# Attention and mixture of experts on one core: the sums of weights behind the centroids' products, and what follows one turn later

## The chip, the cores and the metric

The kernel runs on one core of one Trainium2 chip. The metric is the device time of one execution in microseconds (us); the median of ten executions is 711.23 us. A core has five engines that run their own instruction queues and wait for each other through semaphores: PE (TensorE, matmuls into PSUM), DVE (VectorE), ACT (ScalarE), POOL (GpSimd) and SP (SyncE, which here only issues DMAs). Each engine works through its own queue strictly in order. An instruction that waits therefore holds up everything behind it on its engine.

## The reference

Attention first, over 4 batches, 8 heads, 768 positions and a head size of 64. Queries and keys are assigned to one of 16 centroids of their head, and a query sees only keys of its own centroid:

```python
q_assign = np.argmax(np.einsum('bhsd,hcd->bhsc', q_n, c_n), axis=-1)
k_assign = np.argmax(np.einsum('bhsd,hcd->bhsc', k_n, c_n), axis=-1)
mask = q_assign[:, :, :, None] == k_assign[:, :, None, :]
scores = np.where(mask, scale * np.matmul(q, k.transpose(0, 1, 3, 2)), -1000000000.0)
attn = np.exp(scores - np.max(scores, axis=-1, keepdims=True))
attn = attn / (np.sum(attn, axis=-1, keepdims=True) + 1e-09)
x = np.matmul(attn, v)
```

The result, as 3072 rows of 512, goes to a mixture of 8 experts: a cosine router picks one expert for each row, and the row becomes `gate * (relu(x @ w1[e]) @ w2[e])`. The change touches only the attention part.

## The kernel before, in words

**Pairs, turns, units.** The attention part runs over 16 pairs n = 0 to 15: a batch and two heads. A pair has two groups (the two halves of the queries), and a group has six units (six blocks of 128 keys). The main loop takes two units a turn, so a pair has six turns, `it` = 0 to 5: the first group ends in turn 2, the second in turn 5. The names in the profile are those of the code; L numbers are lines of the kernel before.

**One turn.** Each engine's order is written out by hand: it is the order in which the loop emits instructions (`manual_schedule` over all five). A turn emits, in this order: some loads on SP; `scores` and `expo` of the next turn's two units; `between(n, it)`, which holds everything that isn't plain attention; the routing of early rows in some turns of batches 2 and 3 (`early`); and `attend` for this turn's two units.

- `scores` (L484) makes a unit's scores on PE: four bf16 matmuls that add the mask out of the tile H ("hot" in the profile), then f32 matmuls with qT and kT. The array works as four tiles of 64*64. The result goes to one of two PSUM tiles s_ps.
- `expo` (L495) is the exponential on ACT, out of s_ps into one of five buffers `prob`. A buffer is free when the unit five before has been attended and added up.
- `attend` (L506) multiplies prob with v on PE, in 64*64 tiles, into o_ps. There is one o_ps tile, so it is used by one group after the other. On DVE the same function adds prob into acc (L515 for a group's first two units, L525 after that). When a group ends, ACT copies o_ps to o_sb (L530).
- `unite` (L539) adds the halves of o_sb into o_sum on POOL, in turns 2 and 5.

**What prepares a pair** (`prep_pieces`). "turn0" and "turn1" turn q and k into qT and kT by 32x32 blocks on DVE (L386). "products" multiplies qT and kT with the centroids on PE, in tiles of 128*32 (L396), and turns the result on DVE into asn (L405). "choose" finds the nearest centroid with four DVE instructions (L414 to L417, amax, sel, sel, pm), writes three small copies into cd on ACT (L419, L422), and lets SP issue a transposing DMA from cd into H (L427). H, qT and kT have two buffers each. H of pair n + 1 is first needed in turn 5 of pair n.

**What ends a pair.** `total` sums acc over its partitions on PE, for both groups of the pair before, with matmuls against ones in tiles of 128*32 (L553); DVE turns the sums (L570) and takes the reciprocal (L571), and POOL spreads it with eight small copies to inv2 (L574). `divide` turns inv2 into den (L585) and multiplies o_sum with it into xT (L589) on DVE. `rows` turns xT into xb (L606) and issues four stores on SP into x_rows (L613). The last group's sums are taken alone, with a reciprocal of 384 columns (L562).

**Shared PSUM.** products, total and the router's matmuls share two PSUM banks ("misc"), used alternately. `route_pieces` belongs to the router of a finished batch: its products (L628, copied by ACT at L636) and logits (L641, reduced by DVE at L644) come in the first two pairs of the next batch.

**Order before.** For pairs n > 0: turn 0 has products for n + 1, then the attend, then total of n - 1; turn 1 has choose for n + 1; turn 2 ends with divide of n - 1 and unite; turn 3 has rows of n - 1; turn 4 has turn0 for n + 2, and turn 5 turn1. Pair 0 differs: turns 0 to 2 hold the turns, the products and choose of pair 1.

**Loads.** SP issues the loads of v for n + 1 in turn 2 (eight DMAs), of q for n + 3 in turn 4 and of k in turn 5 (four each), all at the head of their turn. In pairs 11 to 15 it also issues the first experts' weights.

Of the kernel before, what the change touches and what calls it, by code (L numbers as in the profile page):

```python
# [34 lines left out]
def bc(ap, shape, axis):  # L35
    return ap.unsqueeze(axis).to_broadcast(shape)
# [3 lines left out]
def kernel(  # L40
# [136 lines left out]
    def misc():  # L177
        return bank("misc", psM)

    pairs = [(b, hp) for b in range(B) for hp in range(NHP)]  # L180
    NP = len(pairs)
# [131 lines left out]
    def turned_experts():  # L313
        bk = misc()
        for c in range(KD):
            nc.tensor.transpose(
                bk[:, E * c : E * c + E], emb[:, P * c : P * c + P], ident[0:E, 0:E]
            )
        nc.vector.tensor_copy(
            embT[:, :, 0:E], bk[:, 0 : KD * E].rearrange("p (c e) -> p c e", e=E)  # L320
        )
# [210 lines left out]
    def unite(g):  # L532

        n, hq, _ = units[GU * g]
        t = ld[n]
        if hq == 0:
            t["o_sum"] = xp.tile([P, 2, HE], F32, tag="o_sum", name="o_sum", bufs=2)
        add = (nc.gpsimd if n + 1 < NP else nc.vector).tensor_tensor
        add(t["o_sum"][:, hq], t["o_sb"][:, 0], t["o_sb"][:, 1], ALU.add)  # L539

    def total(*gs):

        g = gs[0]
        d = gr[g]
        n = units[GU * g][0]
        G = len(gs)
        bk = misc()

        M, W = (D, HS) if G == 1 else (D // 2, HS // 2)
        for i in range(P // M):  # L550
            for k, g in enumerate(gs):
                c = i * W % HS
                nc.tensor.matmul(  # L553
                    bk[M * i : M * i + M, W * k : W * k + W],
                    lhsT=ones[:, 0:M],
                    rhs=gr[g]["acc"][:, i * W // HS, c : c + W],
                    start=True,
                    stop=True,
                )
        den = d["den"] = smp.tile([P, G, HS], F32, tag="den", name="den", bufs=1)  # L560
        if G == 1:
            nc.vector.reciprocal(den[:, 0], bk[:, 0:W])  # L562
            return


        U = W // SQ
        sums = smp.tile([P, G * U, SQ], F32, tag="sums", name="sums", bufs=1)
        inv = smp.tile([P, G, U], F32, tag="inv", name="inv", bufs=1)
        inv2 = d["inv2"] = smp.tile([P, G, 2, U], F32, tag="inv2", name="inv2", bufs=1)
        nc.vector.transpose(sums.rearrange("p g i -> p (g i)"), bk[:, 0 : G * W])  # L570
        nc.vector.reciprocal(inv.rearrange("p k u -> p (k u)"), sums[:, :, 0])  # L571
        for i in range(4):
            for to in (i, i ^ 1):
                nc.gpsimd.tensor_copy(  # L574
                    inv2[M * to : M * to + M, :, i % 2], inv[M * i : M * i + M]
                )

    def divide(*gs):
        n, hq, _ = units[GU * gs[0]]
        d = gr[gs[0]]  # L580
        G = len(gs)
        if hq == 0:
            xT[pairs[n]] = xp.tile([P, 2, HS], F32, tag="xT", name="xT", bufs=4)
        if G == 2:
            nc.vector.transpose(  # L585
                d["den"].rearrange("p k (u t) -> p (k u) t", t=SQ),
                bc(d["inv2"].rearrange("p k h u -> p (k h u)"), [P, G * HS // SQ, SQ], 2),
            )
        nc.vector.scalar_tensor_tensor(  # L589
            out=xT[pairs[n]][:, hq : hq + G],  # L590
            in0=ld[n]["o_sum"][:, hq : hq + G, 0:HS],
            scalar=ld[n]["o_sum"][:, hq, HS:HE],
            in1=d["den"],
            op0=ALU.add,
            op1=ALU.mult,
        )
        for g in gs:
            gr[g].clear()
# [473 lines left out]
    def expert_of(it):  # L1072
        table = {"early": e_early, "sized": e_sized, "block": e_block, "whole": e_block}[it.kind]
        return nc.values_load(
            table[0:1, it.j : it.j + 1], engines=(EngineType.SP,), min_val=0, max_val=E - 1
        )
# [247 lines left out]
    def piece(n, name, *args):  # L1324
        if n < NP:
            if n not in prepare:
                prepare[n] = prep_pieces(n)
            prepare[n][name](*args)

    def between(n, it):  # L1330
        b, nb = divmod(n, NHP)
        if n == 0:

            if it == 0:
                piece(1, "turn0")
                piece(1, "turn1")
            elif it == 1:
                piece(1, "products")
            elif it == 2:
                piece(1, "choose")  # L1340
                turned_experts()
            elif it == 3:
                later_constants()
        elif it == 0:
            piece(n + 1, "products")
        elif it == 1:
            piece(n + 1, "choose")
        elif it == 3:
            rows(2 * n - 2, 2 * n - 1)
        if it == 4:  # L1350
            piece(n + 2, "turn0")
        elif it == 5:
            piece(n + 2, "turn1")
        if b > 0:
            if nb == 0 and it == 3:
                route[b - 1] = route_pieces(b - 1)
            products, logits, read, norms, choose = route.get(b - 1, (None,) * 5)


            m = NJ * nb + it  # L1360
            if m in (8, 11, 14):
                read((m - 8) // 3 * 2, (m - 8) // 3 * 2 + 2)
            if m in (15, 16, 18, 19, 21, 22):
                norms((15, 16, 18, 19, 21, 22).index(m))
            if (nb, it) == (0, 4):
                products(0)
            elif (nb, it) == (0, 5):
                products(1)
            elif (nb, it) == (1, 2):
                logits(0)  # L1370
            elif (nb, it) == (1, 3):
                logits(1)
            elif (nb, it) == (1, 4):
                choose()
        if n == NP - 1 and it == 4:
            route[b] = route_pieces(b)
            route[b][2](0, NJ, 0, P - SQ)
        first = {
            (11, 3): (w1s, 0, 0),
            (12, 3): (w1s, 0, 1),  # L1380
            (13, 3): (w2s, 0, 0),
            (14, 3): (w2s, 0, 1),
            (14, 4): (w1s, 1, 0),
            (15, 0): (w1s, 1, 1),
            (15, 1): (w2s, 1, 0),
            (15, 2): (w2s, 1, 1),
        }
        if (n, it) in first:
            w, j, i = first[n, it]
            own = E0[j]  # L1390
            if own.e is None:
                own.e = expert_of(own)
            x, chunks = (moe_w1, KD) if w is w1s else (moe_w2, KF)
            load_part(w[own.slot], x, own.e, chunks, i, 2)
# [9 lines left out]
    with tc.manual_schedule(engines=by_hand):  # L1404
        begin()
        for i in range(0, len(units), 2):
            n, it = divmod(i // 2, NJ)

            if n == it == 0:
                load(2, "qk")  # L1410
            if it == 2 and n + 1 < NP:
                load(n + 1, "v")
            if it >= 4 and n + 3 < NP:
                load(n + 3, "qk"[it - 4])
            for m in range(i + 2, min(i + 4, len(units))):
                scores(m)
                expo(m)
            between(n, it)
            if it == 4 and n == NP - 1:
                divide(2 * n)  # L1420
            b, nb = divmod(n, NHP)
            if (b, nb, it) in early:
                early[b, nb, it]()
            if i + 2 == len(units):
                ats.close()
                tile_waits = {"side": "right", "reuse_waits": "tile"}
                psX = ctx.enter_context(tc.tile_pool(name="psX", bufs=1, space=PSUM, **tile_waits))
                turn_x(E0[0], nc.scalar.copy, xp.tile([P, DM], F32, tag="acc", name="xTm", bufs=3))
            for m in range(i, i + 2):
                attend(m)  # L1430
            if it == 2:
                if n > 0:
                    divide(2 * n - 2, 2 * n - 1)
                unite(2 * n)
            elif it == 5:
                unite(2 * n + 1)
            if i + 2 == len(units):
                rows(ngroups - 2)
                route[b][0](0)
            if it == 0 and n > 0:  # L1440
                total(2 * n - 2, 2 * n - 1)
            elif it == 3 and n == NP - 1:
                total(2 * n)
        at.close()
        mop = ctx.enter_context(tc.tile_pool(name="mop", bufs=2, **tile_waits))
# [193 lines left out]
```

## Time and profile before

| what | value |
|---|---|
| median of 10 runs | 711.23 us (711.06 to 712.62) |
| the profiled execution | 711.25 us, its span 709.4 us |
| granted TensorE clock, mean | 0.997 |
| PE busy | 694.8 us (98% of the span) |
| DVE, ACT, POOL busy | 381.2, 268.3, 264.8 us |
| scores L484 (f32 part), 1536 matmuls | 156.1 us |
| attend L506, 1536 matmuls | 142.6 us |
| acc L525 on DVE, 128 instructions | 125.1 us |
| reciprocal spread L574 on POOL, 120 copies | 42.9 us |

The span begins with the first instruction and ends with the last; the time has a little around it. In a timeline a line gives the start in us, the duration, engine, line, operation, what is written and read, and how many instructions were merged; the brackets give the idle time of the engine ahead of it and what ended it. Matmuls of different array tiles run side by side, so durations in a merged line overlap; the distance between starts is the better measure.

### The profile page before, as it was taken

The numbers are of one execution on the slowest core, as the hardware profiler recorded it, in microseconds if no ns is written. First come the engines' busy times: TensorE is split into PE (matmuls) and PEld (weight loads), VectorE is DVE, ScalarE is ACT, GpSimd is POOL, SyncE is SP. The second block draws the span as 40 slices with busy tenths as digits, with TensorE's granted clock in tenths as the row PEclk, the third lists the DMA queues.
The fourth block names the chain that finished last, engine by engine and source line by source line (L and its number), as shares of the span: only waits on it lengthen the run. The fifth ranks groups of instructions, "written<-read, shape, count | busy, mean of one in ns | idle before, by whom it ended". The sixth has DMA issues, their size and how long they took to land.

```text
span 709.4 us, 16021 instructions
## 1 busy us (share of the span) xinstructions
PE 694.8 (98%) x6462; PEld 454.6 (64%) x6462; DVE 381.2 (54%) x665; ACT 268.3 (38%) x454; POOL 264.8 (37%) x402
## 2 busy tenths in 40 slices
PE   6999999999999999999999999999999999999995
PEld 3444444444444444444876668897979797979793
DVE  4788887998979998998684111340120303031210
ACT  4566665577556656666415110101011111111110
POOL 2122222222224221354043546736264454545412
PEclk9999999999999999999999999999999999999998
DMA  9636665866548687769698987268768686869450
GB/s 147 93 63 107 105 104 86 152 146 116 99 75 160 123 158 154 125 190 356 124 340 313 347 322 265 70 247 287 260 211 298 210 301 234 313 243 330 142 197 29
DMA packets 244123, 135.53 MB, mean 191 GB/s; under 512 B 207808, under 2 KB 207810, under 8 KB 244044
## 3 DMA queue, kind: packets, MB, share of 16 engines
q1 hardware_dynamic: 237852, 121.28, 63.9%
q0 software_dynamic: 6016, 13.12, 5.3%
q8 instruction: 53, 0.87, 0.5%
q14 instruction: 26, 0.21, 0.1%
q10 hardware_dynamic: 176, 0.05, 0.0%
HBM read 115.92 MB, written 13.12 MB: 182 GB/s over the span
## 4 chain that ended last, share of the span: by engine, by line
PE 83%; DVE 5%; issue 5%; DMA 4%; POOL 1%; ACT 0%; POOLq 0%; SPq 0%; DVEq 0%; ACTq 0%
PE s_ps L484 19%; PE o_ps L506 16%; PE h_ps L1259 10%; PE y_ps L1275 10%; PE h_ps L1174 9%; PE y_ps L1209 5%; PE misc L1209 5%; PE x_ps L1174 3%; DMA out_dram<-ys,spidx 3%; DVE acc L525 2%; PE misc L553 2%; PE misc L396 2%; PE misc L628 1%; DMA k<-in_k_dram 1%; POOL out_dram L1050 1%
## 5 line engine op out<-in xcount | busy, mean ns | idle before, releaser
L495 ACT ACTIVATE prob<-s_ps 128x768 f32<-128x768 f32 x192 | 153.5, 811 | 93.5 <-PE s_ps L484 72.8
L484 PE MATMUL s_ps<-qT,kT 64*64 64x384 f32 x1536 | 156.1, 482 | 0.0
L506 PE MATMUL o_ps<-prob,v 64*64 64x385 f32 x1536 | 142.6, 487 | 0.0
L525 DVE TENSOR_TENSOR acc<-acc,prob 128x768 f32<-128x768 f32 x128 | 125.1, 977 | 8.5 <-DVE acc L525 0.5
L506 PEld LDWEIGHTS o_ps<-prob,v 64*64 64x64 f32 x1536 | 54.2, 133 | 70.6 <-issue 59.2
L1218 DVE STREAM_TRANSPOSE ys<-y_ps 128x256 f32<-128x256 f32 (+4 forms) x16 | 6.7, 416 | 153.3 <-PE y_ps L1209 153.3
L1259 PEld LDWEIGHTS h_ps<-xTm,w1s 128*128 128x128 f32 x768 | 87.4, 192 | 2.3 <-issue 1.6
L1259 PE MATMUL h_ps<-xTm,w1s 128*128 128x128 f32 x768 | 88.3, 275 | 0.0
L539 POOL TENSOR_TENSOR o_sum<-o_sb 128x385 f32<-128x385 f32 x30 | 32.1, 1071 | 149.5 <-ACT o_sb L530 149.5
L1050 POOL DMA_INDIRECT out_dram<-ys,spidx x56 | 57.0, 1018 | 74.5 <-DVE ys L1234 59.6
L1275 PE MATMUL y_ps<-w2s,hT 128*128 128x512 f32 x192 | 84.5, 593 | 0.0
L484 PEld LDWEIGHTS s_ps<-qT,kT 64*64 64x64 f32 x1536 | 56.4, 133 | 37.6 <-issue 34.6
L1174 PE MATMUL h_ps<-xTs,w1s 128*128 128x272 f32 (+7 forms) x384 | 72.9, 346 | 0.8 <-ACTq L1539 0.8
L1174 PEld LDWEIGHTS h_ps<-xTs,w1s 128*128 128x128 f32 x384 | 66.6, 190 | 8.1 <-issue 2.9
L1266 ACT ACTIVATE hT<-h_ps 128x512 f32<-128x512 f32 x24 | 14.3, 596 | 143.7 <-PE h_ps L1259 143.7
L484 PE MATMUL s_ps<-hot 64*64 64x384 bf16 x768 | 64.9, 325 | 2.3 <-ACT prob L495 1.3
L1039 POOL DMA_INDIRECT xs<-x_rows,gpidx x56 | 57.2, 1021 | 17.1 <-issue 16.8
L574 POOL COPY inv<-inv 32x12 f32<-32x12 f32 x120 | 42.9, 358 | 55.0 <-DVE inv L571 50.6
L1275 PEld LDWEIGHTS y_ps<-w2s,hT 128*128 128x128 f32 x192 | 35.6, 190 | 40.2 <-issue 40.2
L484 PEld LDWEIGHTS <-hot 64*64 64x64 bf16 x768 | 23.8, 107 | 39.7 <-issue 38.4
L1209 PE MATMUL y_ps<-hTs,w2o 128*128 128x272 f32 (+7 forms) x256 | 48.0, 346 | 0.0
L1209 PE MATMUL misc<-hTs,w2o 128*128 128x272 f32 (+7 forms) x256 | 48.0, 346 | 0.0
(264 smaller groups left out, 687.4 us busy)
## 6 DMA issues: line engine op xcount, KB each, us to landing
w1s<-in_moe_w_dram SPq DMA_DIRECT2D x18, 2048.0 KB, 10.6
w2s<-in_moe_w_dram SPq DMA_DIRECT2D x18, 2048.0 KB, 14.5
v<-in_v_dram SPq DMA_DIRECT2D x128, 48.0 KB, 2.1
q<-in_q_dram SPq DMA_DIRECT2D x60, 96.0 KB, 3.5
k<-in_k_dram SPq DMA_DIRECT2D x60, 96.0 KB, 3.5
x_rows<-xb SPq DMA_DIRECT2D x60, 96.0 KB, 2.9
xr<-x_rows SPq DMA_DIRECT2D x9, 512.0 KB, 4.0
w1s<-in_moe_w_dram SPq DMA_DIRECT2D x4, 1024.0 KB, 9.8
```

The lines of the kernel that those rows point to most:

```text
L484: nc.tensor.matmul(s_ps[D * half : D * half + D, h, 0:HS], lhsT=l[rows, half], rhs=r[rows], start=part == (1 if len(parts) < 2 else 0), st ...
L495: nc.scalar.activation(d["prob"][:, :, 0:HS], d["s_ps"][:, :, 0:HS], ACTF.Exp, scale=scale)
L506: nc.tensor.matmul(g["o_ps"][D * h : D * h + D, half, 0:HE], lhsT=ld[n]["v"][keys, j, h], rhs=d["prob"][keys, h, 0:HE], start=(j == 0), st ...
L525: nc.vector.tensor_tensor(g["acc"], g["acc"], d["prob"][:, :, 0:HS], ALU.add)
L539: add(t["o_sum"][:, hq], t["o_sb"][:, 0], t["o_sb"][:, 1], ALU.add)
L574: nc.gpsimd.tensor_copy(inv2[M * to : M * to + M, :, i % 2], inv[M * i : M * i + M])
L1039: nc.gpsimd.indirect_dma_start(out=to, out_offset=None, in_=of, in_offset=bass.IndirectOffsetOnAxis(ap=at, axis=0), bounds_check=n - 1, oo ...
L1050: inst = nc.gpsimd.indirect_dma_start(out=to, out_offset=bass.IndirectOffsetOnAxis(ap=at, axis=0), in_=of, in_offset=None, bounds_check=n - 1,
L1174: nc.tensor.matmul(bk, lhsT=w1s[it.slot][:, c, P * f : P * f + P], rhs=d["xT"][:, c, 0:C], start=(c == 0), stop=(c == KD - 1),)
L1209: nc.tensor.matmul(bks[g][:, 0:C], lhsT=d["w2"][:, f, P * g : P * g + P], rhs=d["hT"][:, f, 0:C], start=(f == 0), stop=(f == KF - 1),)
L1259: nc.tensor.matmul(bk[:, m : m + P], lhsT=w1s[it.slot][:, c, f0 + m : f0 + m + P], rhs=d["xT"][:, P * c : P * c + P], start=(c == 0), stop ...
L1275: nc.tensor.matmul(bk, lhsT=d["hT"][:, P * c : P * c + P], rhs=w2s[it.slot][:, c], start=(c == 0), stop=(c == KF - 1),)
```

## The change

Products for the next pair move from turn 0 to turn 1, and total of the pair before comes directly behind them, ahead of the attend of turn 1. Choose goes from turn 1 to 2, divide from the end of turn 2 to that of turn 3, rows from turn 3 to 4, the turn of q from 4 to 5, the turn of k from 5 to turn 0 of the next pair. The router's products go one turn later too. unite stays in turns 2 and 5.

```diff
         elif it == 0:
+            piece(n + 1, "turn1")
+        elif it == 1:
             piece(n + 1, "products")
-        elif it == 1:
+            total(2 * n - 2, 2 * n - 1)
+        elif it == 2:
             piece(n + 1, "choose")
-        elif it == 3:
+        elif it == 4:
             rows(2 * n - 2, 2 * n - 1)
-        if it == 4:
+        if it == 5:
             piece(n + 2, "turn0")
-        elif it == 5:
-            piece(n + 2, "turn1")
...
-            if (nb, it) == (0, 4):
+            if (nb, it) == (0, 5):
                 products(0)
-            elif (nb, it) == (0, 5):
+            elif (nb, it) == (1, 0):
                 products(1)
...
             if it == 2:
-                if n > 0:
-                    divide(2 * n - 2, 2 * n - 1)
                 unite(2 * n)
+            elif it == 3 and n > 0:
+                divide(2 * n - 2, 2 * n - 1)
             elif it == 5:
                 unite(2 * n + 1)
...
-            if it == 0 and n > 0:
-                total(2 * n - 2, 2 * n - 1)
-            elif it == 3 and n == NP - 1:
+            if it == 3 and n == NP - 1:
                 total(2 * n)
```

## The prediction

> **What bounds the kernel now.** I read the page first, for the engine that carries the time, and then the timeline of the attention part, since the change touches only that (it ends near 338 us).
>
> ```profile
> PE 694.8 (98%) x6462; PEld 454.6 (64%) x6462; DVE 381.2 (54%) x665; ACT 268.3 (38%) x454; POOL 264.8 (37%) x402
> PE 83%; DVE 5%; issue 5%; DMA 4%; POOL 1%; ACT 0%; POOLq 0%; SPq 0%; DVEq 0%; ACTq 0%
> ```
>
> PE sets the end. In the timeline of PE, a turn in which nothing else runs goes from one first matmul of the scores to the next in 2.91 us (182.38 to 185.29). The next view is the timeline of the pair that begins at 195.89: its turn 0, and the head of its turn 1.
>
> ```profile
> 195.89 0.34 PE L484 MATMUL s_ps<-hot 64*64 64x384 bf16 x4
> ...
> 197.62 0.52 PE L396 MATMUL misc<-qT,cnB 128*32 128x384 f32 x2
> ...
> 198.40 1.52 PE L506 MATMUL o_ps<-prob,v 64*64 64x385 f32 x16
> 198.61 0.58 DVE L405 STREAM_TRANSPOSE asn<-misc 128x384 f32<-128x384 f32 x1 [2.69 <-ACT prob L495]
> ...
> 199.85 0.88 PE L553 MATMUL misc<-acc,ones 128*32 128x192 f32 x16
> 200.66 0.36 PE L484 MATMUL s_ps<-hot 64*64 64x384 bf16 x4
> 200.90 0.58 DVE L570 STREAM_TRANSPOSE sums<-misc 128x384 f32<-128x384 f32 x1 [0.87 <-PE misc L553]
> 201.51 0.23 DVE L571 RECIPROCAL inv<-sums 128x12 f32<-128x12 f32 x1
> 201.66 0.50 DVE L414 TENSOR_REDUCE amax<-asn 128x24 f32<-128x384 f32 x1
> ...
> 203.76 0.40 ACT L419 ACTIVATE cd<-pm,wcd 128x24 bf16<-128x24 bf16 x1 [0.41 <-DVE pm L417]
> ```
>
> PE interrupts its 64*64 work twice in turn 0: for the centroids' products (L396) and, behind the attend, for the sums (L553). `choose` starts right behind the reciprocal, and its copies on ACT (L419, L422) come in turn 1, when ACT has nothing urgent behind them. DVE is nearly full here (50.82 us busy of 58.00 between 36 and 94 us); PE is not held up.
>
> The last view is that of the first pair, whose `choose` already stands in turn 2, where the change puts all of them.
>
> ```profile
> 22.66 1.52 PE L506 MATMUL o_ps<-prob,v 64*64 64x385 f32 x16
> ...
> 25.20 0.55 DVE L414 TENSOR_REDUCE amax<-asn 128x24 f32<-128x384 f32 x1
> ...
> 27.36 0.40 ACT L419 ACTIVATE cd<-pm,wcd 128x24 bf16<-128x24 bf16 x1 [0.68 <-DVE pm L417]
> ...
> 28.22 0.80 ACT L530 COPY o_sb<-o_ps 128x770 f32<-128x770 f32 x1
> ...
> 29.08 1.52 PE L506 MATMUL o_ps<-prob,v 64*64 64x385 f32 x16
> ```
>
> The copy of the finished group out of o_ps (L530) stands behind cd on ACT, and the next group's first attend (29.08), which writes the one o_ps tile, starts only when that copy is done.
>
> **The gain: PE enters another shape once instead of twice.** Turns 0 and 1 of a pair take 4.76 + 2.93 us, 1.88 over two plain ones. The matmuls are four passes of 192 columns and two of 384; a pass of 384 takes 0.32 (16 attend matmuls, four passes, in 1.29), so 1.30 is work and 0.58 is going in and out twice, 0.29 a visit. With the sums directly behind the products one visit's 0.29 goes. No row shows the step from products to sums; it costs between 0 and 0.29, and I take 0.02, as the step from bf16 to f32 inside the scores shows next to none: 0.27 saved. There are 14 pairs with both (n = 1 to 14; the last pair has no products): 14 x 0.27 = 3.8 us.
>
> **The loss: choose in turn 2 holds up the copy of o_ps.** Turn 2 is the one whose second unit ends the first group, so its attend is followed by the copy on ACT; `choose` stands before that attend in the program, so cd precedes the copy on ACT. cd waits for DVE, and DVE has in its order now: turn of the products (L405), turn of the sums, reciprocal, two acc of turn 1, and only then choose. Counted from N, the start of the attend in turn 1:
>
> - The chain: sums start at N + 0.17 (323.24 to 323.41 in the last pair), 0.61 to the reciprocal, 0.15 to acc, 2.05 for two acc, 2.10 from choose to cd (201.66 to 203.76), 0.86 to the copy (27.36 to 28.22), 0.80 for it, 0.06 to the matmul (29.02 to 29.08): N + 6.80.
> - PE without a wait: 1.35 to turn 2 (22.66 to 24.01), 2.91 to turn 3, 1.62 through its scores to the attend (182.38 to 184.00): N + 5.88.
>
> PE is held 0.92 us. A held attend also costs 0.05 more: in the first pair I work out a wait of 0.04 and the turn is 0.10 longer (3.01 against 2.91). So 0.97. The two acc are taken from the last pair, where they follow the reciprocal directly and the eight copies of inv run on POOL meanwhile, as they will everywhere:
>
> ```profile
> 324.02 0.23 DVE L571 RECIPROCAL inv<-sums 128x12 f32<-128x12 f32 x1
> 324.17 4.16 DVE L525 TENSOR_TENSOR acc<-acc,prob 128x768 f32<-128x768 f32 x4
> 324.31 4.30 POOL L574 COPY inv<-inv 32x12 f32<-32x12 f32 x8 [1.49 <-DVE inv L571]
> ```
>
> The lower bound is the first pair's own chain, without sums and without POOL: 29.08 - 22.66 = 6.42, so 0.54 + 0.05. This holds in full for n = 1 to 4, 6 to 8 and 10 to 12: 10 x 0.97 = 9.7. Pairs 5, 9 and 13 have logits (L641, 0.63 a turn) in turns 2 and 3 ahead of that attend; these 1.26 us of PE work cover the wait. Pair 14 has the early items' tokens (0.54) there: 0.4 is left. Together 10.1 us.
>
> Here a rule of the Trainium skill speaks against the change. On the page "SBUF — State Buffer", section "Who interferes with whom", a VectorE instruction with two SBUF inputs and a GpSimd instruction that reads SBUF exclude each other, and the one that comes second blocks fully. The rows above agree that they disturb each other, but here GpSimd is the one that loses: its eight copies take 4.30 instead of 3.07 us, an acc 1.04 instead of 0.97. Were each of the two acc held a whole copy of 0.38 us, the sum would be some 7 us higher.
>
> **What is given back.** Pairs 10 to 12 carry the early items' routing on DVE and wait for it now: the turns at 236.02, 244.24, 253.44 and 256.56 are 0.53, 0.48, 0.21 and 1.18 over their like, 2.4 us. A hold frees DVE's backlog, and DVE's work is spread better: xb moves to turn 4, the turns of q and k to 5 and 0. Following DVE through these pairs in its new order, the first acc of pair 10's turn 5 ends at N + 17.05, where the exp that takes its prob buffer should have begun at N + 16.7 (0.34 late), and the next choose starts 0.47 late. That leaves 0.8, a gain of 1.6. The bound on the other side: no gain.
>
> **What moves at no cost.** In an ordinary pair DVE does 17.9 us of work, and the pair will last 20 us; kT is there at N + 16.5 and the products ask for it at N + 19.1, or at N + 18.1 without the hold. The divide (1.97) goes to turn 3: inv's copies on POOL, at worst 4.30 long, end at N + 5.4 and den is due at N + 7.8. `unite` now stands before it, on another buffer of o_sum. H's transposing DMA goes one turn later: issued at N + 5.9, 3.2 us to landing, so there at N + 9.2; turn 5's scores ask for it at N + 10.9 with the hold. If that cover of 1.7 went, each 0.1 would cost 1.3 us over the pairs. On SP the eight loads of v now stand ahead of it, but they wait for nothing and are issued before turn 1's end. q's loads pass ahead of the four stores of rows, k's stay behind; both are used over a pair later. route's products (0.93 each) and their copies on ACT keep their cost one turn later, and the first pair only shifts turns. The last pair's xb falls behind the 2.56 us reciprocal, so DVE ends attention about 1.3 us later; PE asks for its last acc 2.0 us after it is done (340.5 and 342.51). At worst this costs 1.3.
>
> **Sum.** The profiled execution took 711.25 us (span 709.4), beside a median of 711.23, so no correction: 711.25 - 3.8 + 10.1 - 1.6 = 716.0.
>
> **Rivals.** (1) The hold is hidden: cd doesn't delay the copy, or choose gets through by N + 5.9 as the copy needs. Then -3.8 and -2.4 of backlog remain: 705.1. It decides at 0.92 us less on the chain. For it speaks only that DVE had idle time in turn 0; against it the first pair, where the delay is to be seen even with 0.5 us of extra PE work (L316) as cover. (2) The switch is not saved: products and sums need a drain between them: 716.0 + 3.8 = 719.8. Nothing shows two such groups side by side. (3) The hold is only the first pair's 0.59, 5.9 in all, with the saving and the relief as above: 711.8, no measurable change. Against it stand the 0.76 us of sums and reciprocal now inside the chain. (4) DVE or H becomes late as well, acc held by POOL's copies being the likeliest: with 0.38 more per acc in 11 pairs, 8 us, 724. Against it the last pair's rows.
>
> PE's new pauses of 0.9 us could also touch its clock. The rows say no: between 239 and 263 us PE paused up to 1.18 us and the granted clock was 1.00. The Trainium skill, page "TensorE: Matmul & The Clock Gate", section "A second HAM failure mode: psum-queue depth-cycling", tells of short, frequent pauses that make the clock swing; here that would make every pair slower than summed. The row decides: nothing added.
>
> **How the numbers follow.** Forecast 0.68, rival 1 0.09, rival 2 0.10, rival 3 0.08, rival 4 0.05. The forecast's own range, from the lower hold with full saving (711.25 - 4.1 + 5.9 - 1.6 = 711.4) to the full hold with neither saving nor relief (721.4). The range for 8 in 10 drops most of rivals 1 and 4 and the corner where all goes badly: 711.0 to 720.0. A measurement tells 0.2% (1.4 us) from no change: faster is rival 1 and a little of 3, 0.11; within it most of 3 and the low end of the forecast, 0.08; slower the rest, 0.81.
>
> **What would show it.** In the profile after: L553 directly behind L396 with no 64*64 matmul between, and turns 0 and 1 together 7.4 instead of 7.7; o_ps (L506) of turn 3 waiting for ACT o_sb, about 0.9 us, in the pairs without logits and none in 5, 9 and 13; on ACT cd with a wait for DVE pm just ahead of L530; little wait left around 236 to 262 us of before. I am wrong if the attend of turn 3 starts 1.62 us into its turn everywhere, or if hot is waited for in turn 5.

## The result: 0.77% slower, and where the time went

The changed kernel takes 717.48 us (median), and the kernel before 712.17 us on the same chips. The ratio is 1.0077, 95% interval 1.0065 to 1.0089. The profiled execution took 716.12 us (span 714.2), against 711.25 us (span 709.4) before. That is 4.9 us more, and 716.0 was forecast. Executions of both kernels differ by 1.4 us and more, the longer ones with a lower mean granted clock (0.992 to 0.996 instead of 0.996 to 0.998; last section), which is why the median of before is 712.17 here and 711.23 further up. PE is no longer always busy, as the page of the changed kernel shows in its sums of busy time and in its chain:

```profile
PE 693.1 (97%) x6462; PEld 464.6 (65%) x6462; DVE 382.6 (54%) x665; ACT 267.8 (37%) x454; POOL 278.4 (39%) x402
PE 74%; DVE 11%; issue 5%; DMA 5%; ACT 2%; POOL 1%; SPq 1%; POOLq 0%; DVEq 0%; ACTq 0%
```

Before, PE held 83% of the chain, DVE 5% and ACT nothing. Nine points of it have gone from PE, mostly to DVE and ACT. The view of the waits of PE names the place:

```profile
PE o_ps L506 <- ACT o_sb L530: 6.6, 10, 0.9
```

The columns are the total in us, the number of waits and the longest one. The first matmul of an attend waited ten times for the copy of o_ps, for up to 0.9 us. Before, the view of PE has no such line. It counts only the time in which PE is idle (0.63 us in the row of pair 2 below, where the turn grows by 0.86), so the sizes below are read from the turns. The timeline of pair 2 of the changed kernel, from its turn 1 to the attend of turn 3, shows the whole chain:

```profile
60.73 0.52 PE L396 MATMUL misc<-qT,cnB 128*32 128x384 f32 x2
...
61.40 0.87 PE L553 MATMUL misc<-acc,ones 128*32 128x192 f32 x16
...
62.20 1.52 PE L506 MATMUL o_ps<-prob,v 64*64 64x385 f32 x16
62.35 0.58 DVE L570 STREAM_TRANSPOSE sums<-misc 128x384 f32<-128x384 f32 x1
62.97 0.23 DVE L571 RECIPROCAL inv<-sums 128x12 f32<-128x12 f32 x1
63.11 1.98 DVE L525 TENSOR_TENSOR acc<-acc,prob 128x768 f32<-128x768 f32 x2
63.26 3.57 POOL L574 COPY inv<-inv 32x12 f32<-32x12 f32 x8 [4.92 <-DVE inv L571]
...
65.02 0.54 DVE L414 TENSOR_REDUCE amax<-asn 128x24 f32<-128x384 f32 x1
...
67.16 0.41 ACT L419 ACTIVATE cd<-pm,wcd 128x24 bf16<-128x24 bf16 x1 [0.95 <-DVE pm L417]
...
68.02 0.80 ACT L530 COPY o_sb<-o_ps 128x770 f32<-128x770 f32 x1
...
68.88 1.52 PE L506 MATMUL o_ps<-prob,v 64*64 64x385 f32 x16 [0.63 <-ACT o_sb L530]
```

The sums follow the products after 0.67 us, with no other shape between. Then choose waits on DVE behind sums, reciprocal and two acc. cd waits on ACT for choose, the copy of o_ps stands behind cd, and PE gets to the attend 6.68 us after N = 62.20 instead of 5.88, 0.80 later; the turn grows by another 0.06.

The attention part repeats almost to the hundredth of a microsecond, so its turns can be compared one by one. I measure a turn on PE from its first matmul of the scores to that of the next turn. Ordinary pair 2, in us:

| turn | 0 | 1 | 2 | 3 | 4 | 5 | pair |
|---|---|---|---|---|---|---|---|
| before | 4.76 | 2.93 | 2.91 | 2.91 | 2.91 | 2.91 | 19.33 |
| after | 2.91 | 4.54 | 2.91 | 3.77 | 2.91 | 2.91 | 19.94 |

Turn 3 is 0.86 longer, in eight of the ten pairs that were forecast to have the hold in full. Of the other two, pair 11 has 1.16 and pair 12 has 0.89. Pairs 5, 9 and 13, whose logits cover the chain, have none, and pair 14 has 0.29. The part behind attention (from the last attend's matmul to the end of PE) is unchanged, 364.1 against 364.2 us.

### The profile page after: what moved, and what is told of

Its sections match the earlier page's. It is cut to its first block, busy times and chain, and to the rows that moved or that the text cites. A ratio compares the mean times of both kernels' runs of the same rounds, so it can differ in the third digit from the quotient of the medians.

```text
span 714.2 us, 16031 instructions
## 1 busy us (share of the span) xinstructions
PE 693.1 (97%) x6462; PEld 464.6 (65%) x6462; DVE 382.6 (54%) x665; ACT 267.8 (37%) x454; POOL 278.4 (39%) x402
## 4 chain that ended last, share of the span: by engine, by line
PE 74%; DVE 11%; issue 5%; DMA 5%; ACT 2%; POOL 1%; SPq 1%; POOLq 0%; DVEq 0%; ACTq 0%
PE s_ps L484 14%; PE o_ps L506 12%; PE h_ps L1259 10%; PE y_ps L1275 10%; PE h_ps L1174 9%; PE misc L1209 5%; PE y_ps L1209 5%; DVE acc L525 4%; PE x_ps L1174 3%; DMA out_dram<-ys,spidx 3%; PE misc L396 2%; PE misc L553 2%; ACT o_sb L530 1%; DVE sel L415 1%; DVE pm L417 1%
## 5 line engine op out<-in xcount | busy, mean ns | idle before, releaser
L506 PEld LDWEIGHTS o_ps<-prob,v 64*64 64x64 f32 x1536 | 56.8, 132 | 73.0 <-issue 54.3
L484 PEld LDWEIGHTS s_ps<-qT,kT 64*64 64x64 f32 x1536 | 59.3, 133 | 38.5 <-issue 36.6
L539 POOL TENSOR_TENSOR o_sum<-o_sb 128x385 f32<-128x385 f32 x30 | 37.2, 1239 | 120.9 <-ACT o_sb L530 120.9
L574 POOL COPY inv<-inv 32x12 f32<-32x12 f32 x120 | 50.3, 419 | 77.5 <-DVE inv L571 73.1
```

The lines of the kernel that those rows point to most:

```text
L484: nc.tensor.matmul(s_ps[D * half : D * half + D, h, 0:HS], lhsT=l[rows, half], rhs=r[rows], start=part == (1 if len(parts) < 2 else 0), st ...
L506: nc.tensor.matmul(g["o_ps"][D * h : D * h + D, half, 0:HE], lhsT=ld[n]["v"][keys, j, h], rhs=d["prob"][keys, h, 0:HE], start=(j == 0), st ...
L574: nc.gpsimd.tensor_copy(inv2[M * to : M * to + M, :, i % 2], inv[M * i : M * i + M])
```

## Experiments

The theory: (a) merging the two visits saves 0.24 us a pair; (b) the time is lost because cd, late from DVE, stands ahead of the copy of o_ps in ACT's queue. The rivals: the hold comes from DVE's accumulation or its buffers, from the turn in which choose stands, or from another of the moved pieces; and H may take the hold's place.

Three remarks on the numbers. Pair 0's first turn takes 1.3 to 2.6 us more where PE's clock falls in it (last section), so pairs 1 to 14 are compared by their turns. The kernels marked "second chip" ran on a chip on which all kernels were slower, the one before 720.99 us; the part behind attention took 7 to 12 us longer there, so only turns and ratios are read from it. And the L numbers are those of each run's own kernel, up to 6 above those of the kernel before.

### Both halves: merging alone, and moving alone

**Merging alone.** The kernel before with

```diff
             piece(n + 1, "products")
+            total(2 * n - 2, 2 * n - 1)
...
-            if it == 0 and n > 0:
-                total(2 * n - 2, 2 * n - 1)
-            elif it == 3 and n == NP - 1:
+            if it == 3 and n == NP - 1:
```

> The kernel before, with one edit: the sums stand directly behind the products in turn 0 instead of behind that turn's attend; nothing is moved to a later turn. Theory: turns 0 and 1 of an ordinary pair take 7.45 instead of 7.69 us, as in the changed kernel, and turn 3 stays 2.91, since choose and cd stay in turn 1. But the sums now ask in turn 0 at 2.4 us for the last acc of the pair before; in ordinary pairs that is done 0.4 us earlier, in pairs 6, 10, 11, 12 and 14, where DVE is behind, it is 1.0 to 2.0 us late. So -0.24 in nine pairs or so, and + 1 to 1.5 in five: 711 to 714 us in all. Rival (the 0.24 comes from the other moves, not from the missing switch): turns 0 and 1 stay at 7.69.

Measured: 714.42 us against 712.51, ratio 1.0029 (1.0018 to 1.0040). An ordinary pair takes 19.08 us (turns 0 and 1: 4.54 and 2.91), 0.245 less than before, in nine of the 14 pairs. In pairs 6, 10, 11, 12 and 14 the sums wait for the last acc, and turn 0 is 0.95 to 1.28 longer than before. The timeline of pair 6 shows it:

```profile
135.47 2.61 DVE L525 TENSOR_TENSOR acc<-acc,prob 128x768 f32<-128x768 f32 x2
...
138.13 0.88 PE L553 MATMUL misc<-acc,ones 128*32 128x192 f32 x14 [0.69 <-DVE acc L525]
```

So (a) holds, and the saving does not need the other moves. It also shows what the later turn gives: by turn 1 the acc has long been done.

**Moving alone.** The changed kernel with the sums behind the attend of turn 1:

```diff
             piece(n + 1, "products")
-            total(2 * n - 2, 2 * n - 1)
...
-            if it == 3 and n == NP - 1:
+            if it == 1 and n > 0:
+                total(2 * n - 2, 2 * n - 1)
+            elif it == 3 and n == NP - 1:
```

> The changed kernel, but the sums stand behind the attend of turn 1 instead of directly behind the products: everything is one turn later, nothing is merged. Theory: PE switches twice again, so turns 0 and 1 take 7.69; DVE adds its two acc of turn 1 before it waits for the sums, and the attend on PE runs meanwhile, so the chain from the attend's start N is 0.15 + 0.5 + 1.9 + 0.61 + 0.15 + 2.14 + 0.86 + 0.80 + 0.06 = 7.2 against 6.85 on PE: turn 3 is 3.25 to 3.3 instead of 3.77. Sum: 14 x 0.245 - 10 x 0.5, about 714.4 us. Rival (the hold comes from the turn that choose stands in alone, wherever the sums are): turn 3 stays 3.77 and the time is 716.1 + 3.4 = 719.5.

Measured in one execution: turns 0 to 3 of pair 2 take 2.91, 4.77, 2.93 and 3.26 us. The turns are those of the theory. The time, 719.91 us, is by chance near the rival's, for other reasons: 1.4 us of the lower clock in pair 0's first turn, 1.8 more in pairs 10 to 14 than the theory's terms give there, where DVE is behind, and 1.9 behind the last attend, where PE now waits for DVE. These three were not foreseen; the theory's 714.4 did not hold for the whole, only its turns.

**Choose alone in turn 2.** The kernel before with

```diff
-        elif it == 1:
+        elif it == 2:
             piece(n + 1, "choose")
```

> The kernel before with choose alone moved from turn 1 to turn 2; the sums stay behind the attend of turn 0. Theory (it takes both, choose in turn 2 and the sums as late as turn 1): counted from the end of the sums, the chain through two acc, choose, cd and the copy takes 6.8 us, and PE has all of turns 1 and 2 and the scores of turn 3 for it, 7.45: turn 3 stays 2.91, no hold, 711.2 us like the kernel before. Rival (choose in the turn in which a group ends is what costs): turn 3 grows by some 0.8 in ten pairs, 719.

Measured in one execution on the second chip: in pairs 1 to 10 no turn differs from the kernel before by more than 0.01 us; turn 3 is 2.91. Only in pair 11, where DVE is behind, is turn 3 0.25 longer, while turn 2 loses its 0.48. (The whole took 721.94 us, where the kernel before had 720.99; 1.7 of that is the lower clock in pair 0.) Choose in the turn in which a group ends costs nothing in ordinary pairs when the sums come a turn earlier. The hold needs both.

### ACT's queue: longer, out of the way, elsewhere

**cd made longer.** The changed kernel with

```diff
             nc.scalar.activation(cd[..., 1], pm, ACTF.Copy, scale=wcd)
+            for _ in range(2 if n > 1 else 0):
+                nc.scalar.activation(cd[..., 1], pm, ACTF.Copy, scale=wcd)
```

> The changed kernel with the first of cd's copies on ACT made three times instead of once, for pairs 2 to 15; two more at 0.22 us from start to start are 0.44. Theory: ACT's copies stand in the chain from choose to the attend of turn 3, so turn 3 grows by 0.44, from 3.77 to 4.2, in the eleven pairs with a hold; in pairs 5, 9 and 13, where logits give 0.46 of slack, next to nothing. 716.1 + 11 x 0.44 = about 721 us. Rival (DVE's accumulation holds PE, ACT only waits beside it): unchanged, 716.

Measured in one execution: 725.75 us. Turn 3 of an ordinary pair is 4.64, 0.87 longer than in the changed kernel, and in pairs 5, 9 and 13 it grew by 0.43 to 0.45. The timeline of pair 2:

```profile
68.46 0.41 ACT L419 ACTIVATE cd<-pm,wcd 128x24 bf16<-128x24 bf16 x1 [0.95 <-DVE pm L417]
68.89 0.83 ACT L421 ACTIVATE cd<-pm,wcd 128x24 bf16<-128x24 bf16 x2
69.55 0.61 ACT L424 ACTIVATE cd<-pm 64x24 bf16<-64x24 bf16 x2
70.18 0.80 ACT L532 COPY o_sb<-o_ps 128x770 f32<-128x770 f32 x1
...
71.04 1.20 PE L508 MATMUL o_ps<-prob,v 64*64 64x385 f32 x12 [1.50 <-ACT o_sb L532]
```

The added copies write the same elements as the first, and they come 0.43 apart from start to start, not 0.22, so the size was wrong; that this is the reason was not tried apart. What they add to ACT's queue, about 0.87, is added to turn 3 one for one. Pairs with logits have 0.87 - 0.44 = 0.43 of slack left, near the 0.46 worked out. ACT's queue carries the hold.

**cd behind the copy.** The changed kernel with the ACT part of choose as a piece of its own, "write", behind the attend:

```diff
             if it == 2:
+                if n > 0:
+                    piece(n + 1, "write")
                 unite(2 * n)
```

> The changed kernel, but the three small copies of cd on ACT, and the transposing DMA of H behind them, are emitted behind the attend of turn 2, so that ACT copies o_ps (L530) first. Theory (the hold is cd standing ahead of that copy in ACT's queue): turn 3 falls from 3.77 to 2.91 us in the pairs without logits, also in pairs 10 to 12 and 14; the 9.2 us of holds go, the merging's 3.4 stays: about 707 us, faster than before. H is issued at N + 6.1 and lands at N + 9.3; turn 5's scores ask at N + 10.1, so no wait for hot. Rival A (the attend of turn 3 is late for another reason: DVE's order, prob, divide in turn 3): turn 3 stays 3.77 and the time about 716. Rival B (H becomes late once the hold is gone): turn 3 is 2.91, turn 5 grows by what H is late.

Measured: 714.59 us against 712.51, ratio 1.0033 (1.0021 to 1.0045), less than the changed kernel's 1.0077 but no gain. The hold is gone from turn 3 in every pair; pairs 2 to 4 and 8 take the full saving (pair 2: 19.08). But in pairs 6, 7 and 14 the scores of turn 5 wait for H: turn 4 grows by 1.22, 0.90 and 1.58. Pair 7:

```profile
169.22 1.41 SPq L432 DMA_TRANSPOSE hot<-cd  x1
...
170.73 3.13 SPq L208 DMA_DIRECT2D q<-in_q_dram  x4
...
174.08 0.36 PE L490 MATMUL s_ps<-hot 64*64 64x384 bf16 x4 [0.72 <-DMA hot<-cd]
```

H's DMA lands after 3.2 to 5.0 us here (median 4.1), not always 3.2 as before. So rival B is right beside the theory: without the hold the DMA has too little time in some pairs. Why it sometimes takes longer was not tried. And pairs 11 and 12 wait for DVE again: their turns 1 are 1.24 and 0.89 us longer than an ordinary merged turn, their turns 0 0.43 and 1.05 longer than a plain one.

**All of choose in turn 1.** The changed kernel with choose, cd's copies too, directly behind the sums:

```diff
             total(2 * n - 2, 2 * n - 1)
-        elif it == 2:
             piece(n + 1, "choose")
```

> The changed kernel with all of choose, its copies of cd too, directly behind the sums in turn 1. Theory: pm comes at N + 3.0, when ACT has turn 2's exps due from N + 2.3; they stand behind cd and start at N + 3.9. The first scores of turn 3, due at N + 4.3, wait for the first of them until 4.75, so about 0.5 in turn 2 or 3 in the ten pairs without logits, instead of the 0.86 of the changed kernel: 716.1 - 10 x 0.36, about 712.5 us. Rival (only the copy of o_ps matters): no hold at all, as with cd in turn 2, 707 to 709.

Measured in one execution on the second chip: turn 3 is 2.91, and turn 2 of ordinary pairs is 3.39, 0.48 longer (in pair 7 1.10): the scores of turn 3 wait for the exps that stand behind cd. That is the theory's place and size; its time can't be compared (728.05 us there).

### Choose earlier on DVE

**Choose ahead of both acc, cd in turn 2:**

```diff
             total(2 * n - 2, 2 * n - 1)
-        elif it == 2:
             piece(n + 1, "choose")
+        elif it == 2:
+            piece(n + 1, "write")
```

> The changed kernel with choose on DVE directly behind the sums in turn 1, ahead of that turn's two acc; the copies of cd and H's DMA stay where the change has them, in turn 2 ahead of the attend. Theory (the hold is length of the chain, because two acc and the sums stand ahead of choose): pm is ready at N + 3.0, cd runs from 3.9 to 4.8 behind turn 2's exps, the copy of o_ps ends at 5.6, before PE asks at 5.9: turn 3 is 2.91 everywhere, turns 0 and 1 stay 7.45. H is issued 1.3 us earlier than with cd behind the copy, so its 3.2 to 5.0 us fit before turn 5 asks at N + 10.1, and no turn 4 or 5 grows. 716.1 - 9.2, less DVE backlog of 1 to 2 us that shows again in pairs 11 and 12: 707 to 709 us. Rival (the place of cd ahead of the copy of o_ps costs by itself, whenever choose is done): turn 3 stays above 3 us and the time above 713.

Measured on the second chip: 729.31 us against 720.99, ratio 1.0109 (1.0082 to 1.0137). Turn 3 is still 3.58 in pair 2, and what it gains in pairs 1 to 9 is lost in pairs 10 to 14: pairs 1 to 14 take 288.2 us together, as in the changed kernel (288.1). I was wrong. The timeline of the same kernel with ranks moved (below) shows why, in pair 2:

```profile
65.13 4.17 DVE L531 TENSOR_TENSOR acc<-acc,prob 128x768 f32<-128x768 f32 x4
...
66.17 0.81 ACT L501 ACTIVATE prob<-s_ps 128x768 f32<-128x768 f32 x1 [0.67 <-DVE acc L531]
...
67.01 0.40 ACT L424 ACTIVATE cd<-pm,wcd 128x24 bf16<-128x24 bf16 x1
...
67.87 0.80 ACT L536 COPY o_sb<-o_ps 128x770 f32<-128x770 f32 x1
```

pm is ready by now, but the second exp of turn 2 waits 0.67 us for a prob buffer, which the first acc frees, and that acc now stands behind choose. cd and the copy of o_ps stand behind that exp. The rival's number was right and its reason open; the next runs decide.

**Ranks in turn 1.** The same kernel with

```diff
-        (2, 2, 0): pa.ranks,
+        (2, 2, 1): pa.ranks,
```

> The kernel with choose early, and the early items' ranks in turn 1 of pair 10 instead of turn 0, that is behind products and sums. In the changed kernel these two matmuls made turn 0 of pair 10 0.77 us longer: a switch to 128*128 of their own, and 0.36 of waiting for cumx on POOL. Theory: in turn 1 they cost 0.20, as in the kernel before, so 0.56 less than the kernel with choose early. Rival: DVE, which then copies the ranks ahead of two acc in its fullest turn, gives it back in turn 3: no difference.

Measured on the second chip: 726.77 us, ratio 1.0104 (1.0063 to 1.0145), which tells nothing against 1.0109. By turns, pair 10 takes 19.96 instead of 20.81 us, 0.86 less and more than the 0.56 expected.

**Choose between the two acc.** The kernel of the last run, with choose taken from behind the sums to between the two attends of turn 1:

```diff
             total(2 * n - 2, 2 * n - 1)
-            piece(n + 1, "choose")
...
-            for m in range(i, i + 2):
-                attend(m)
+            attend(i)
+            if it == 1 and n > 0:
+                piece(n + 1, "choose")
+            attend(i + 1)
```

> The changed kernel with choose on DVE between the two acc of turn 1, cd's copies in turn 2 as changed, and ranks in turn 1 of pair 10. With choose ahead of both acc, the second exp of turn 2 waited for the first acc of turn 1 (the prob buffer), and cd and the copy of o_ps stood behind that exp on ACT. Theory (whatever stands ahead of the copy on ACT counts, an exp too): now the first acc ends at N + 1.9, in time for that exp at 3.1; pm comes at N + 4.0, cd ends at 4.9, the copy at 5.7, PE asks at 5.9. Turn 3 is 2.91 to 2.95, turns 0 and 1 stay 7.45, H lands by N + 8.2 to 10.0 and isn't waited for. The DVE backlog shows again in turns 1 of pairs 11 and 12, some 2 us. About 1.5 to 2.5 us less than the kernel before, ratio 0.997. Rival (choose anywhere after the products' turn holds the copy): turn 3 stays above 3.3.

Measured: 710.62 us against 712.49, ratio 0.9969 (0.9957 to 0.9980): faster than both kernels. Turn 3 is no longer than in the kernel before in any pair but 11 (0.10 more); turns 0 and 1 of pair 2 are 2.91 and 4.54, and the pair takes 19.08. Turns 1 of pairs 11 and 12 are together 2.1 us longer than ordinary ones, as expected, but their turns 0 another 1.5, where the kernel before loses 2.4 in these pairs. So of the 3.4 us that merging saves 1.9 are left in pairs 1 to 14. Pair 2, counted from N = 62.86:

```profile
62.86 1.52 PE L512 MATMUL o_ps<-prob,v 64*64 64x385 f32 x16
...
63.77 0.90 DVE L531 TENSOR_TENSOR acc<-acc,prob 128x768 f32<-128x768 f32 x1
...
64.58 0.55 DVE L415 TENSOR_REDUCE amax<-asn 128x24 f32<-128x384 f32 x1
...
65.32 1.56 ACT L501 ACTIVATE prob<-s_ps 128x768 f32<-128x768 f32 x2 [2.36 <-PE s_ps L490]
...
66.90 0.40 ACT L424 ACTIVATE cd<-pm,wcd 128x24 bf16<-128x24 bf16 x1
...
67.77 0.80 ACT L536 COPY o_sb<-o_ps 128x770 f32<-128x770 f32 x1
...
68.73 1.47 PE L512 MATMUL o_ps<-prob,v 64*64 64x385 f32 x16
```

The two exps run without a wait, cd follows them, and the copy ends at 68.57, N + 5.71; the attend starts at N + 5.87, on PE's own time. cd is still ahead of the copy on ACT, so its place alone does not cost: what counts is when the queue up to the copy is through. That refutes the last rival.

**A sixth prob buffer.** The kernel with choose ahead of both acc and ranks in turn 1, and six buffers; and, as a control, the kernel before with six:

```diff
-    emb = smp.tile([E, DM], F32, name="emb", bufs=1)
+    emb = smp.tile([P, S], F32, tag="den", name="emb", bufs=1)[0:E, 0:DM]
...
-    probs = [pp.tile([P, 2, HS + 4], F32, name=f"prob{i}") for i in range(5)]
+    probs = [pp.tile([P, 2, HS + 4], F32, name=f"prob{i}") for i in range(6)]
```

> The kernel with choose ahead of both acc, cd in turn 2, ranks in turn 1, and a sixth prob buffer (its room is taken from the experts' embedding, which now shares the buffer of den). Theory (the hold left there was the exp waiting for the first acc of turn 1): with six buffers that exp needs an acc of the turn before, so turn 3 falls from 3.58 to 2.91 and turns 0 and 1 stay 7.45; pairs 10 to 12 lose most of their waits for acc. 711.25 - 3.4 - 2.4 + 1: about 706.5, ratio 0.993. Rival (DVE is the bound of these pairs, more buffers only move the wait): turn 3 is 2.91 but turns 0 or 1 grow, ratio 1.0.

> The kernel before with the same sixth prob buffer and nothing else: how much the buffer gives by itself. Theory: ordinary pairs have no wait for acc and stay 19.32 us; the 2.4 us of waits in pairs 10 to 12 go, so 709, ratio 0.997. Rival (those waits are DVE's work itself): no change.

Measured: 709.64 us, ratio 0.9971 (0.9962 to 0.9980), and for the control 711.91 us, ratio 1.0005 (0.9994 to 1.0015). With six buffers turn 3 falls from 3.59 to 2.91: the exp's wait for the buffer was the rest of the hold, as the theory says. Pairs 10 to 12, however, keep their waits: turn 1 of pair 12 is 2.2 us longer than an ordinary merged turn, and in the control the 0.2 that turn 5 of pair 11 loses comes back in turn 0 of pair 12. With six buffers PE waits there for the turn of k on DVE, which the change has put only one turn ahead of the products: in pair 12 PE stands idle for 1.42 us until the products of kT begin at 260.98, just after kT is ready (260.92). In the control they begin just after kT too (258.92 and 258.87). There DVE's work itself is the bound, and the gain expected there did not come.

## Why the prediction was right

**The saving, 3.8 us forecast.** It measured 14 x 0.245 = 3.4. Merging alone shows the same 0.245. 0.02 was taken for the step from products to sums; it is 0.045, as two visits cost 0.29 each.

**The hold, 10.1 us.** It measured 9.2 in turns 3: seven times 0.84 to 0.87 in pairs 1 to 4 and 6 to 8, 0.86, 1.16 and 0.89 in pairs 10 to 12, and 0.29 in pair 14. Place, cause, the exception of the pairs with logits and the smaller hold of pair 14 were as forecast. The term that was too large is the two acc: 2.05 was taken from the last pair, and here 1.91 pass from the first acc to choose (63.11 to 65.02). The acc are no faster, 0.90 and 0.98 us in both places; but in the last pair a third acc follows, 0.10 after the end of the second, while choose starts 0.07 before that end. This made the chain 6.68 instead of 6.80. The extra cost of a held attend, put at 0.05, is 0.06.

On the rule of the Trainium skill (page "SBUF — State Buffer", section "Who interferes with whom"): the eight copies on POOL took 3.57 us, beginning beside the two acc, and 3.07 before, where they began beside choose. The trace agrees for a copy that comes second: the first of them starts 0.15 us after an acc and ends 0.05 us after it, taking 0.80 us instead of the 0.19 of a copy that meets no acc. The two acc, 1.98 together, took no longer than two without copies beside them (1.98 at 55.64). So GpSimd waits, and the 7 us that were worked out for the other case did not come.

**The relief, 1.6 us.** The four waits of 2.4 us in pairs 11 and 12 went. Of new ones in these pairs the forecast had one of 0.34 and a choose 0.47 late. The trace has turn 1 longer by 0.28, 0.27 and 0.37 in pairs 10, 11 and 12, and the 0.3 above the ordinary hold in turn 3 of pair 11, already counted above. So the relief without that is 1.5. The size came out by luck in part, for the places did not: pair 10's turn 5 waits for nothing. In pair 12 the products of kT wait for DVE's turn of k and begin just after it ends (266.76 and 266.70); the forecast that kT is there in time holds for ordinary pairs alone.

**What was missed.** ranks, two small matmuls of the early items in turn 0 of pair 10, had shared PE's visit with the products. The products moved and they did not, so they now make a visit of their own, and wait for POOL:

```profile
219.62 2.71 POOL L687 TENSOR_TENSOR cumx<-cumx,eq 128x8 bf16<-128x8 bf16 x5
...
222.38 0.21 PE L769 MATMUL misc<-cumx,onesb 128*128 128x104 bf16 x1 [0.36 <-DMA x_rows<-xb]
```

Turn 0 of pair 10 takes 3.68 us, 0.77 over a plain one, where they had cost 0.20: 0.56 lost. In the timeline the matmul starts just after the cumx that it reads, though the wait is put down to another release. The part on early items counted DVE's work in these pairs and forgot PE's. Sum: -3.4 + 9.2 - 1.5 + 0.6 = 4.9, as measured; 4.7 was forecast, with errors of opposite sign. The mechanism was right, but that 716.0 lies so near the 716.12 of the profiled execution is partly luck.

**The rivals.** The hold is not hidden (1), the switch is saved (2), the hold is above the first pair's 0.59 (3), and acc is not held up by POOL (4). The cover of H, put at 1.7 us, sufficed with the hold. With cd behind the copy and no hold it went, and H cost 3.7 us in three pairs, since its DMA then took up to 5.0 us.

## What to carry to other kernels

When a step moves later in a tuned order, follow each queue that it crosses to the next thing that another engine waits for. Here the step on DVE fed a small copy on ACT, and the copy that frees PSUM stood behind it: 0.24 us saved on PE cost 0.86 there, while choose between the two acc kept the saving in ordinary pairs. Small matmuls that share another group's visit on PE should be moved together with it: ranks cost 0.20 us beside the products and 0.77 alone, 0.36 of it a wait. Where one wait is taken away, work out how much time the next has: the DMA of H and the buffer of prob came up as soon as the copy was out of the way.

## What the runs showed of the hardware that was not expected

PE's clock falls to half in some executions for 3.4 us (6.8 in one) just as attention begins, and in others of the same chip it does not. These are the lines for 16 to 22 us of the kernel with choose between the acc, and then of the one with six buffers; the third column from the right is the granted clock:

```profile
16.00:22.00 6.00, 5.12 (x56) 2.76 (x59) 4.08 (x12) 3.14 (x4) 0.00 (x0) 0.72 1.12 113
```

```profile
16.00:22.00 6.00, 5.25 (x76) 2.75 (x72) 3.80 (x10) 4.07 (x6) 0.00 (x0) 1.00 1.13 112
```

In the first, turn 0 of pair 0 is 1.27 us longer. Once PE has begun, no single pause before the fall is longer than 1.7 us (1.65, ending at 7.15 us in the kernel with cd behind the copy, waiting for k), and one of 1.69 in the kernel with cd made longer was followed by no fall. The last three, of 0.6 to 1.1 us between 13 and 17.5 us, are there in executions without the fall too. The Trainium skill, page "TensorE: Matmul & The Clock Gate", section "What's actually happening", puts the fall after an idle window of about 3.4 us; here several shorter pauses were followed by it. Why it comes in some executions and not in others was not tried.
